# Tiles 0 and 1 of a two-block layer: normalise before the transpose, k weights in two row halves, and an order of work written as a table

## The chip, the cores and the metric

The kernel runs on one core of one Trainium2 chip. The metric is the time of one execution on the device in microseconds (us), as a median over runs. The core has five engines with a queue of instructions each: TensorE (PE: matmuls and the transposes that are matmuls with an identity), VectorE (DVE), ScalarE (ACT), GpSimd (POOL) and SyncE (SP), which issues most of the DMAs. Engines meet only through semaphores. Data live in SBUF (128 partitions), and matmul results in the 8 banks of PSUM.

## The reference

2048 rows of 512 bf16 numbers pass through two blocks with a residual each: linear attention with 32 heads of 16, and a gated MLP that mixes along the rows.

```python
def _A_ref(x, wqkv, wo):                     # x is already layer-normalised
    qkv = (x @ wqkv) ...                      # q, k, v in 32 heads of 16
    phi = lambda t: jnp.where(t > 0, t + 1, jnp.exp(t)) + 1e-06
    pq, pk = phi(q), phi(k)
    kv = jnp.einsum('bhsd,bhse->bhde', pk, v)
    z = jnp.einsum('bhsd->bhd', pk)
    num = jnp.einsum('bhqd,bhde->bhqe', pq, kv)
    den = jnp.einsum('bhqd,bhd->bhq', pq, z)[..., None] + 1e-06
    return (num / den) ... @ wo

def _B_ref(x, w_in, w_sp, b_sp, w_out):      # x is already layer-normalised
    z = _gelu(x @ w_in); z1, z2 = z[..., :896], _layernorm(z[..., 896:])
    g = jnp.einsum('ts,bsf->btf', w_sp, z2) + b_sp[None, :, None]
    return (z1 * g) @ w_out

h = x + _A_ref(_layernorm(x), wqkv, wo)
out = h + _B_ref(_layernorm(h), w_in, w_sp, b_sp, w_out)
```

## The kernel before

The 2048 rows are 16 tiles of 128. Everything stays in SBUF between the blocks. The program is written as a list of operations (`op`), each with an engine, what it reads and writes, a cost that a planner uses, and a due time `want`. `schedule` then goes through a model of the five engines and the DMA queue, and on each engine takes as next the operation with the smallest sum of possible start and half its due time; the due times are a list of 729 numbers (`WANT`) that replaces those written in the code. So the order of each engine's queue comes from the planner before the program is built. `fillers` then puts dummy matmuls with constants (L578) in front of those early matmuls for which the planner sees TensorE idle for more than 0.35 us, up to the first outer product. `waits` places the semaphores.

The order of the work at the start, which is what the change touches:

- SP loads x tile 0, tile 1, tiles 2 and 3, then the k columns of `wqkv` ("wk", 512 rows by 512, in one DMA of 512 KB), three more pairs of x tiles, the q columns ("wq"), one transposing load of the spatial weights `w_sp` (L1043), two DMA transposes of normalised tiles ("tx", L675), the last three pairs of x tiles, and so on.
- VectorE takes mean and variance of each x tile (L590, L594). ScalarE turns the variance into 1/std with Ln and Exp (L605, L607). VectorE, for some tiles ScalarE, writes the normalised tile `xn` (L617, L625).
- Tiles 0 and 1 (`LATE`) are special. VectorE only subtracts their mean (`xc`, L657). TensorE transposes the centred tile (L686), ScalarE and VectorE copy a half each out of PSUM (L691, L693), TensorE multiplies the transposed tile with the k weights (L747), and 1/std comes in as the scale by row of ScalarE's Exp and Relu (L716, L722). Their normalised `xn` is written too, later; a DMA transpose puts it into `xT`, where the q projection reads it.
- Tiles 2 and 3 (`PE_X`) are normalised, transposed on TensorE (L635) and copied by ScalarE (L701). Their 1/std is worked out for both in one pair of instructions. Tiles 4 to 15 are normalised and transposed by DMA (L675), whose result TensorE multiplies with the k weights (L758).
- The feature map of k: Exp and Relu on ScalarE, then minimum and sum on VectorE (L718, L724). `xk` (L768) adds, over all tiles, the products of `xn` with it into 4 banks of PSUM. q (L860) is computed for groups of four tiles: the first group reads the transposed tiles 0 to 3 and the q weights.

Behind this come the sums by head (L780), the product with the v and output weights (L813, L829), the output of the attention (L905, L912) with its division by way of a reciprocal that DMAs spread over partitions (L886) and that VectorE applies (L892), the second normalisation, the two halves of the MLP's first product (L968, L1023), the mixing along rows (L1063) and the last product with its residual (L1083, L1087, stores L1090).

A DMA's queue is served in the order of its issues. `dma_start` on SP or on ScalarE each has a queue of its own; before, ScalarE's is used only for one of the last stores. A tile that VectorE or ScalarE writes for a DMA transpose must be complete before SP issues it, and all that stands behind it on SP waits along.

## Time and profile before

| | us |
|---|---|
| median of 3 runs | 242.42 |
| lowest, highest | 241.86, 245.08 |
| span of the profiled execution, first to last instruction | 240.8 |
| TensorE busy in it | 235.3 |
| VectorE busy | 127.1 |
| ScalarE busy | 83.9 |
| first transpose on TensorE starts | 4.84 |
| first k matmul starts | 6.80 |
| first q matmul starts | 13.04 |

The profiled execution's own time is known by its span alone, 240.8 us, which is 1.62 us under the median. In the profile "PE" is TensorE's matmuls and "PEld" its weight loads, which run beside them. "SPq" and "ACTq" are the issues of DMAs. A row of a timeline gives start and length in us, engine, line, operation, output and input, how many instructions are merged in it, and in brackets how long the engine idled before and what ended that. Ends of matmuls are modelled: a row of several ends later than the next can start. A line number is that of the kernel before unless it is said to be the changed kernel's.

### The profile page before, as it was taken

The page shows a single profiled execution, that of the slowest core. Times are in us where ns is not written, and L with a number is a line of the kernel's source. Part 1 is how long each engine was busy: PE and PEld are TensorE (multiplying, and loading weights), DVE is VectorE, ACT ScalarE, POOL GpSimd, SP SyncE. Part 2 cuts the span into 40 slices and gives each one's busy share as a digit, 9 for nine tenths or more (in the row PEclk, how much of TensorE's full clock was granted, in tenths as well). Part 3 has the DMA queues.
Part 4 walks back from the last instruction along what each step waited for, and adds up shares of the span by engine and source line. Part 5 has one row for each costly group of instructions (what it writes and reads, how often), then busy time and mean ns, then how long its engine had stood idle before and what let it go on. Part 6 is the DMA issues. An engine that isn't in the chain of part 4 may idle for free.

```text
span 240.8 us, 3056 instructions
## 1 busy us (share of the span) xinstructions
PE 235.3 (98%) x1177; PEld 108.4 (45%) x1199; DVE 127.1 (53%) x269; ACT 83.9 (35%) x132; POOL 13.9 (6%) x33
## 2 busy tenths in 40 slices
PE   8999999999999999999999999999999999999996
PEld 2434445454344544444444444444444444444443
DVE  4999856399999983226222333324333433322443
ACT  4888975566065799994111100000000000000000
POOL 3000000000102160213000000000000000000000
PEclk9999999999999999999999999999999999999999
DMA  6986559632542555444444449463300001000022
GB/s 197 254 224 91 109 114 355 207 112 81 145 125 44 92 107 101 97 88 89 109 92 104 88 92 237 108 89 88 109 0 0 25 22 44 0 3 0 0 87 87
DMA packets 61805, 24.18 MB, mean 100 GB/s; under 512 B 52064, under 2 KB 61152, under 8 KB 61792
## 3 DMA queue, kind: packets, MB, share of 16 engines
q1 hardware_dynamic: 61648, 23.97, 41.3%
q8 instruction: 9, 0.15, 0.3%
q10 hardware_dynamic: 144, 0.03, 0.1%
q14 instruction: 4, 0.03, 0.1%
HBM read 7.47 MB, written 2.10 MB: 40 GB/s over the span
## 4 chain that ended last, share of the span: by engine, by line
PE 87%; DMA 5%; DVE 3%; ACT 2%; SPq 1%; issue 1%; ACTq 0%
PE ps L1063 40%; PE ps L1083 10%; PE ps L968 10%; PE ps L1023 10%; PE ps L768 4%; PE ps L860 4%; DMA xT_pq_z<-k_xn_z 4%; PE ps L905 3%; PE ps L758 3%; PE ps L578 2%; DMA wsp<-e 1%; ACT e L716 1%; SPq L886 1%; DVE xT_pq_z L727 1%; ACT k_xn_z L836 1%
## 5 line engine op out<-in xcount | busy, mean ns | idle before, releaser
L1063 PE MATMUL ps<-wsp,k_xn_z 128*128 128x512 bf16 x328 | 73.6, 379 | 0.4
L1069 DVE TENSOR_TENSOR e<-ps,e 128x512 bf16<-128x512 f32 x28 | 19.4, 692 | 69.2 <-PE ps L1063 69.2
L1063 PEld LDWEIGHTS ps<-wsp,k_xn_z 128*128 128x128 bf16 x336 | 32.8, 98 | 39.8 <-issue 0.4
L1023 PE MATMUL ps<-hT,win 128*128 128x512 bf16 x110 | 26.0, 379 | 0.1
L968 PE MATMUL ps<-win,hT 128*128 128x384 bf16 (+1 forms) x126 | 25.3, 352 | 0.1
L1083 PE MATMUL ps<-wout,xT_pq_z 128*128 128x512 bf16 (+2 forms) x125 | 25.1, 355 | 0.1
L1063 PE MATMUL ps<-wqkv_wsp,k_xn_z 128*128 128x512 bf16 x110 | 24.2, 379 | 0.1
L1028 ACT ACTIVATE xT_pq_z<-ps 128x1024 bf16<-128x1024 f32 x14 | 14.1, 1023 | 25.6 <-PE ps L1023 25.5
L590 DVE BATCH_NORM_STATS2 small<-xh 128x6 f32<-128x512 bf16 x32 | 21.0, 679 | 3.1 <-DMA xh<-in_A_x_dram 3.0
L968 PEld LDWEIGHTS ps<-win,hT 128*128 128x128 bf16 x128 | 12.5, 98 | 12.4
L1083 PEld LDWEIGHTS ps<-wout,xT_pq_z 128*128 128x128 bf16 x126 | 11.8, 98 | 12.7
L1063 PEld LDWEIGHTS ps<-wqkv_wsp,k_xn_z 128*128 128x128 bf16 x112 | 11.0, 98 | 13.2
L1023 PEld LDWEIGHTS ps<-hT,win 128*128 128x128 bf16 x112 | 10.9, 98 | 12.7 <-DVE xh L924 0.3
L1087 DVE TENSOR_TENSOR e<-ps,xh 128x512 bf16<-128x512 f32 (+2 forms) x18 | 11.4, 633 | 9.7 <-PE ps L1083 9.2
L716 ACT ACTIVATE e<-ps 128x1024 bf16<-128x1024 f32 (+1 forms) x16 | 15.4, 973 | 2.4 <-PE ps L860 1.2
L860 PE MATMUL ps<-xT_pq_z,wqkv_wsp 128*128 128x512 bf16 x61 | 15.0, 379 | 0.6 <-DMA xT_pq_z<-k_xn_z 0.5
L768 PE MATMUL ps<-k_xn_z 128*128 128x512 bf16 x63 | 15.2, 379 | 0.2 <-issue 0.2
L975 ACT ACTIVATE k_xn_z<-ps 128x896 bf16<-128x896 f32 x12 | 10.9, 909 | 8.8 <-PE ps L968 8.8
L905 PE MATMUL ps<-k_xn_z,xT_pq_z 128*128 128x512 bf16 x58 | 13.3, 380 | 0.3 <-DVE xT_pq_z L892 0.3
L758 PE MATMUL ps<-wqkv_wsp,xT_pq_z 128*128 128x512 bf16 x55 | 13.2, 379 | 0.2 <-ACT xT_pq_z L701 0.2
L1071 DVE TENSOR_TENSOR xT_pq_z<-xT_pq_z,e 128x512 bf16<-128x512 bf16 x28 | 11.9, 425 | 2.2 <-ACT xT_pq_z L1028 1.3
L979 ACT ACTIVATE e<-k_xn_z 128x896 bf16<-128x896 bf16 x12 | 11.4, 951 | 0.3
(77 smaller groups left out, 169.4 us busy)
## 6 DMA issues: line engine op xcount, KB each, us to landing
wsp<-e SPq DMA_DIRECT2D x16, 128.0 KB
out_dram<-e SPq DMA_DIRECT2D x15, 128.0 KB, 1.7
xh<-in_A_x_dram SPq DMA_DIRECT2D x7, 256.0 KB, 3.8
win<-in_B_w_in_dram SPq DMA_DIRECT2D x1, 1792.0 KB, 7.3
wqkv_wsp<-in_A_wqkv_dram SPq DMA_DIRECT2D x3, 512.0 KB, 7.2
wout<-in_B_w_out_dram SPq DMA_DIRECT2D x1, 896.0 KB, 5.5
wsp<-in_B_w_sp_dram SPq DMA_TRANSPOSE x48, 2.6
wqkv_wsp<-in_A_wo_dram SPq DMA_DIRECT2D x1, 512.0 KB, 5.2
```

Source lines behind the costliest of these rows:

```text
L590: op("dve", (0.577, 0.69), lambda e: e.bn_stats(row[0:6].ap(), src.ap()), r=[src], w=[row[0:6]], want=want, name=name)
L716: first = op("act", act_c(n, ptr=len(pt)), lambda e: e.activation(e_(ev).ap(), src(t), ACT.Exp, scale=sc), r=[t()] + pt, w=[e_()], want=wa ...
L758: i = e.matmul(t(bank(ti)).ap(), lhsT=lhs.ap()[:, c, :], rhs=rhs.ap()[:, c, :], start=(c == 0), stop=(c == KD - 1))
L768: i = e.matmul(HT(bank(j)).ap(), lhsT=xn[n, j * P:(j + 1) * P].ap(), rhs=pk[n, :].ap(), start=(n == 0), stop=(n == NT - 1))
L860: k = e.matmul(t(bank(i)).ap(), lhsT=lhs.ap()[:, c, :], rhs=rhs.ap()[:, c, :], start=(c == 0), stop=(c == KD - 1))
L905: i = e.matmul(t(bank(ti)).ap(), lhsT=l.ap()[:, c, :], rhs=mw[c, :].ap(), start=(c == 0), stop=(c == KD - 1 and not unit))
L968: k = e.matmul(t(bank(i)).ap()[:, 0:b - a], lhsT=l.ap()[:, c, :], rhs=win[c, a:b].ap(), start=(c == 0), stop=(c == KD - 1))
L1023: k = e.matmul(t(bank(i)).ap(), lhsT=l.ap()[:, c, :], rhs=r_.ap()[:, c, :], start=(c == 0), stop=(c == KD - 1))
L1028: op("act", act_c(1024), lambda e: e.activation(d.ap(), t(None if same else flat).ap(), ACT.Gelu_apprx_tanh), r=[t()], w=[d], want=want + ...
L1063: k = e.matmul(t(bank(0)).ap(), lhsT=l.ap()[:, s - a, :], rhs=r_.ap()[:, s - a, :], start=(s == 0), stop=(s == NT - 1))
L1069: op("dve", dve_c(512), lambda e: e.tensor_tensor(gb().ap(), t(bank(0)).ap(), bsp().ap()[:, tg * GW:(tg + 1) * GW], ALU.add), r=[t(), bsp( ...
L1083: k = e.matmul(t(bank(0)).ap()[:, 0:r_.ap().shape[-1]], lhsT=l.ap()[:, fc, :], rhs=r_.ap()[:, fc, :], start=(fc == 0), stop=(fc == KF - 1))
```

## The change

- Tiles 0 and 1 (now `FIRST`) are no longer centred only. Each is normalised by VectorE as soon as ScalarE has its 1/std; the normalised tile is transposed on TensorE, and the two copies out of PSUM go into `xT` itself. The buffers `xc` and `xcT`, the two centring instructions, the scale by row in Exp and Relu, and the two DMA transposes of tiles 0 and 1 go.
- 1/std of tiles 2 and 3 is worked out for each by itself (one pair of ScalarE instructions more).
- The k weights come in two DMAs of 256 KB, a row half each ("wka", "wkb"): the first on ScalarE's queue, behind the table load in ScalarE's order and ahead of all else there, the second on SP behind x tiles 0 to 3. k of tiles 0 and 1 is two operations, one for each half.
- The planner no longer chooses: the order of each engine is a table (`ORDER`) of operation numbers. The model behind it, from which the number of fillers and the places in PSUM follow, has other constants for DMAs.
- By the table, these places change. On SP: wkb, tiles 6 and 7, tiles 4 and 5, wq, then the other four pairs of x tiles, two loads of `w_sp`, then the DMA transposes of tiles 4, 5, 7, 6, the v weights (they stood behind the MLP's first weights before), and those of 10, 11, 8, 9, 15, 12, 14, 13; the output weights come after five of the spreading DMAs. On TensorE: 9 fillers, transpose of tile 0, 1 filler, transpose of tile 1, k of tile 0, transpose of tile 2, k of tile 1, transpose of tile 3, k of 2 and 3, xk of tile 0, then half of the first q, xk of tile 1, the other half, xk of tile 2, k of 4 and 5 (before: 9 fillers, transposes of 0 and 1 with 2 fillers between, k of 0 and 1, transposes of 2 and 3, 1 filler, k of 2 and 3, xk of 0, all of the first q, xk of 1 and 2, k of 4 and 5). From the middle of the attention on, single operations change places with a neighbour; from the MLP's first product on, TensorE's order is the same but for tiles 2 and 3 changing places.

```diff
-    LATE = (0, 1)
+    FIRST = (0, 1)
-    LN1 = [[0], [1], [2, 3], [4, 5, 6, 7], [8, 9, 10, 11], [12, 13, 14, 15]]
+    LN1 = [[0], [1], [2], [3], [4, 5, 6, 7], [8, 9, 10, 11], [12, 13, 14, 15]]
...
-    load("sp", "wk", wqkv[:, D:2 * D], w3[:, :, D:2 * D], D * D * 2, -29)
+    load("act", "wka", wqkv[0:2, D:2 * D], w3[:, 0:2, D:2 * D], D * D, -29)
+    load("sp", "wkb", wqkv[2:4, D:2 * D], w3[:, 2:4, D:2 * D], D * D, -29)
...
-                op("dve", dve_f(512), lambda e, n=n, d=d, m=m: e.tensor_scalar(d.ap(), x[n, :].ap(), m.ap(), None,
-                                                                              op0=ALU.subtract),
-                   r=[x[n, :], m], w=[d, cT[n]()], want=T1(n) - 3, name=f"xc{n}")
...
-                                  xc[n][c * P:(c + 1) * P].ap(), ident.all().ap())
+                                  xn[n, c * P:(c + 1) * P].ap(), ident.all().ap())
...
-        d0, d1 = xcT[n][0:2, :], xcT[n][2:4, :]
+        d0, d1 = xT[0:2, n * P:(n + 1) * P], xT[2:4, n * P:(n + 1) * P]
...
-        dma_t(xn[n, :], xT[:, n * P:(n + 1) * P], 12, f"tx{n}")
...
-        first = op("act", act_c(n, ptr=len(pt)), lambda e: e.activation(e_(ev).ap(), src(t), ACT.Exp, scale=sc),
+        first = op("act", act_c(n), lambda e: e.activation(e_(ev).ap(), src(t), ACT.Exp),
...
-            lhs = xcT[n].all() if n in LATE else xT[:, n * P:(n + 1) * P]
...
+            halves = ((0, 2), (2, 4)) if n in FIRST else ((0, 4),)
+            for a, b in halves:
+                l, rhs = xT[a:b, n * P:(n + 1) * P], wqkv[a:b, D:2 * D]
...
-    g.schedule()
+    g.schedule(ORDER)
```

More of the change, by code (lines that the diff above doesn't have):

```diff
@@ L149, in ready, with schedule @@
         return p.done
-    def schedule(self):
+    def schedule(self, table):
+        queue = {e: [self.ops[i] for i in table[e]] for e in self.ENGINES}
+        assert sorted(i for e in self.ENGINES for i in table[e]) == list(range(len(self.ops)))
+        assert all(o.eng == e for e in self.ENGINES for o in queue[e])
         for o in self.ops:
@@ L235, in schedule @@
                     o.done = t_end + 0.3
[L236 to L240 removed]
+                elif o.eng == "act":
+                    a_beg = max(t + LAG, a_end)
+                    a_end = a_beg + o.nbytes / SHARE
+                    o.done = a_end + LAND
+                else:
+                    c_end = max(t + LAG, c_end, t_end + 1.2)
+                    left_ = o.nbytes
+                    for until, rate in ([(a_end, SHARE)] if c_end >= a_beg - 0.3 else []) + RATES:
+                        if left_ > 0 and c_end < until:
+                            k = min(left_, (until - c_end) * rate)
+                            c_end += k / rate
+                            left_ -= k
+                    o.done = c_end + LAND
             for tl in o.tiles:
@@ L253, in schedule @@
                 last = o
-            order[o.eng].append(o)
-            cand[o.eng].remove(o)
-            for u in users.get(o, ()):
-                need[u] -= 1
-                if not need[u]:
-                    cand[u.eng].append(u)
             left -= 1
-        self.order = order
+        self.order = queue
         self.span = max(o.done for o in self.ops)
@@ L1101, in build @@
     g.outs = outs
-    if WANT is not None:
-        for o, w in zip(g.ops, WANT):
-            o.want = w * UNIT
     return g
```

143 lines of the change are left out of this document (60 added, 83 removed), and 73 rows, old and new, of tables (ORDER, WANT).

## The prediction

> **What bounds the kernel now.** I read the page first: engines, then the chain that ended last.
>
> ```profile
> PE 235.3 (98%) x1177; PEld 108.4 (45%) x1199; DVE 127.1 (53%) x269; ACT 83.9 (35%) x132; POOL 13.9 (6%) x33
> ...
> PE 87%; DMA 5%; DVE 3%; ACT 2%; SPq 1%; issue 1%; ACTq 0%
> ```
>
> TensorE is busy for 98% of a 240.8 us span and makes 87% of the chain. The matrix work is not changed, so only time in which TensorE idles or runs fillers can be won. The windows view says where that lies (columns: stretch, length, then busy time and instructions by engine).
>
> ```profile
> 0.00:4.83 4.83, 4.00 (x9) 1.18 (x10) 1.84 (x6) 1.79 (x4) 2.01 (x13) 1.00 0.56 153
> ...
> 6.80:13.04 6.24, 5.58 (x32) 2.34 (x30) 6.22 (x21) 5.92 (x14) 0.00 (x0) 1.00 1.26 250
> 13.04:54.00 40.96, 40.59 (x264) 18.96 (x269) 29.56 (x62) 29.27 (x41) 0.00 (x0) 1.00 0.66 171
> 54.00:65.00 11.00, 10.57 (x53) 4.37 (x51) 10.36 (x18) 4.86 (x7) 0.96 (x2) 1.00 0.36 112
> 65.00:238.60 173.60, 172.69 (x818) 80.62 (x832) 76.94 (x162) 41.21 (x66) 10.93 (x18) 1.00 0.32 73
> ```
>
> From 13.04 us on TensorE idles 0.37, 0.43 and 0.91 us, mostly cracks of 0.05. What can be won lies before 13.04. There VectorE is busy 6.22 of 6.24 us and ScalarE 5.92. TensorE's timeline and the list of its waits:
>
> ```profile
> 0.83 4.00 PE L578 MATMUL ps<-const-bfloat16-1.0 128*128 128x512 bf16 x9 [0.83 <-PEq L1174]
> 4.84 0.59 PE L686 MATMUL ps<-small,hn 128*128 128x128 bf16 x4
> 5.22 1.06 PE L578 MATMUL ps<-const-bfloat16-1.0 128*128 128x512 bf16 x2
> 6.40 0.59 PE L686 MATMUL ps<-small,hn 128*128 128x128 bf16 x4
> 6.80 1.91 PE L747 MATMUL ps<-wqkv_wsp,hn 128*128 128x512 bf16 x8
> 8.68 0.72 PE L635 MATMUL ps<-small,k_xn_z 128*128 128x128 bf16 x8
> 9.24 0.38 PE L578 MATMUL ps<-const-bfloat16-1.0 128*128 128x512 bf16 x1
> 9.77 1.90 PE L758 MATMUL ps<-wqkv_wsp,xT_pq_z 128*128 128x512 bf16 x8 [0.15 <-ACT xT_pq_z L701]
> 11.50 1.03 PE L768 MATMUL ps<-k_xn_z 128*128 128x512 bf16 x4
> 13.04 3.61 PE L860 MATMUL ps<-xT_pq_z,wqkv_wsp 128*128 128x512 bf16 x15 [0.51 <-DMA xT_pq_z<-k_xn_z]
> ...
> 20.80 1.89 PE L758 MATMUL ps<-wqkv_wsp,xT_pq_z 128*128 128x512 bf16 x8
> ```
> ```profile
> PE ps L860 <- DMA xT_pq_z<-k_xn_z: 0.5, 1, 0.5
> PE ps L905 <- DVE xT_pq_z L892: 0.3, 1, 0.3
> ```
>
> L686 are the transposes of tiles 0 and 1, L747 k of both, L635 and L758 the same of tiles 2 and 3, L768 the first outer product (xk0), L860 q of the first group. From the first k matmul to q, 6.24 us pass, with 20 matmuls and 8 transposes in them: 20 x 0.216 ((11.50 - 9.77) / 8) + 0.56 (8.68 to 9.24) = 4.88. So 1.36 us are lost there: a wait for xn2, a filler, 0.15 for a copy, and 0.51 at 13.04 for the DMA transposes of tiles 0 and 1, which only the change removes.
>
> **The change, part by part.** The rows that set the start:
>
> ```profile
> 0.79 1.28 ACT L572 ACT_TABLE_LOAD   x1 [0.79 <-PEq L1174]
> ...
> 2.96 0.69 DVE L590 BATCH_NORM_STATS2 small<-xh 128x6 f32<-128x512 bf16 x1 [2.96 <-DMA xh<-in_A_x_dram]
> 3.69 0.18 DVE L594 BATCH_NORM_AGGREGATE small<-small 128x2 f32<-128x6 f32 x1
> ...
> 3.91 0.30 ACT L605 ACTIVATE small<-small 128x1 f32<-128x1 f32 x1 [1.83 <-DVE small L594]
> 4.23 0.20 ACT L607 ACTIVATE small<-small 128x1 f32<-128x1 f32 x1
> ...
> 4.37 0.33 DVE L657 TENSOR_SCALAR hn<-xh,small 128x512 bf16<-128x512 bf16 x1
> ...
> 5.47 0.29 DVE L693 COPY hn<-ps 128x256 bf16<-128x256 bf16 x1
> 5.67 0.41 DVE L617 TENSOR_SCALAR k_xn_z<-xh,small 128x512 bf16<-128x512 bf16 x1
> 6.00 0.35 DVE L657 TENSOR_SCALAR hn<-xh,small 128x512 bf16<-128x512 bf16 x1
> ...
> 7.03 0.29 DVE L693 COPY hn<-ps 128x256 bf16<-128x256 bf16 x1
> ...
> 7.32 0.38 DVE L617 TENSOR_SCALAR k_xn_z<-xh,small 128x512 bf16<-128x512 bf16 x1
> ...
> 9.11 1.09 ACT L701 ACTIVATE xT_pq_z<-ps 128x512 bf16<-128x512 bf16 x2
> ```
>
> *k weights on two queues.* No run shows two load queues at once. The half on ScalarE's queue leaves beside x0 and shares the DMA engines with it. The rate in the first 5 us, in slices of 0.125 us:
>
> ```profile
> GB/s 0 0 0 0 0 0 0 0 0 0 0 0 0 0 90 115 164 230 279 254 221 287 336 197 123 147 57 172 270 369 369 344 279 213 229 246 303 369 393 377
> ```
>
> 128 KB at the top rate of 393 is 0.33 us: if x0 must let as many bytes of weights pass, it lands up to 0.33 later. It lands no later at all if ScalarE's issue waits behind its table load (0.79 + 1.28), and hardly so if the engines' gaps (57 to 230 GB/s) take the weights in. I take +0.25, nearer the shared end, since both queues are free at 0.79. The Trainium skill ("DMA: Bandwidth & Descriptors", Issuing engines are not separate DMA queues) speaks against a second queue: it says that loads from two engines end on the same 16 DMA engines and interleave, so that only issue time is saved. By that rule the term is the full 0.33; no run here shows it yet. The weights themselves are in time either way: k waits for nothing at 6.80.
>
> *Normalise at once.* Stats at 3.21, aggregate 0.73 later (3.69 - 2.96) at 3.94, ScalarE's Ln and Exp end 0.74 after that (4.23 + 0.20 - 3.69) at 4.68, xn0 4.70 to 5.11 (0.41). Before, the centring needed no ScalarE but stood behind the second stats until 4.37, so tr0 comes at 5.16 in place of 4.84. Copies follow 0.63 later (5.47 - 4.84) at 5.79; xn1 0.20 behind (5.67 - 5.47), 5.99 to 6.40; tr1 at 6.45 (before 6.40: 6.00 + 0.35 + 0.05). k0 then starts 0.40 later, at 6.85 for 6.80: **0.05 lost**. VectorE drops two centrings (0.33 + 0.35) and moves two normalises ahead of them; that brings tile 2 forward. Exp and Relu of tiles 0 and 1 lose their scale by row; I count that at nothing, since TensorE waits there for the copies, not for them. The memsets and masks on GpSimd change places only: its part of the start is 2.01 us long by the first row of the windows, and done before the first Ln wants its constant. The constants of the planner and the table of orders cost no instruction; what they move is counted where it lands.
>
> *Tiles 2 and 3.* Copies of tile 1 at 7.08, xn2 0.29 behind (7.32 - 7.03) to 7.78, tr2 at 7.83, where k0 has ended at 7.71: 0.12 waited. k1 8.11 to 8.97, tr3, k2 at 9.25 to 10.12. ScalarE has one more Ln/Exp pair (0.53) for tile 3, then the first Relu, the copy of tile 2 by about 9.15, and that of tile 3 at 9.6 to 10.2 (0.6 each: 1.09 for two): k3 waits about 0.13, like the 0.15 in the row. k3 and xk0 (0.865 each) end at 11.98. xk0 needs the first feature sum from VectorE by 11.1; I get 11.0.
>
> *No DMA transposes of tiles 0 and 1.* SP's queue:
>
> ```profile
> 6.13 4.08 SPq L675 DMA_TRANSPOSE xT_pq_z<-k_xn_z  x2
> 10.25 1.62 SPq L540 DMA_DIRECT2D xh<-in_A_x_dram  x3
> 11.91 2.45 SPq L1043 DMA_TRANSPOSE wsp<-in_B_w_sp_dram  x2
> 14.41 11.10 SPq L675 DMA_TRANSPOSE xT_pq_z<-k_xn_z  x8
> ```
>
> They held SP for 4.08 us and the last three x loads behind them until 10.25; these now leave right behind wq. q no longer waits for a transpose, only for its weights, which land earlier in the byte order than now. So q starts at 11.98 for 13.04: **1.06 won**.
>
> *Is it kept?* Behind q TensorE is full, so the lead lasts if every supplier moves too. ScalarE's and VectorE's work follows TensorE's and moves with it. The DMA transposes are the close ones. The summary of those issued from 14 to 26 us:
>
> ```profile
> L675 SPq DMA_TRANSPOSE xT_pq_z<-k_xn_z x8: 1264/1272/1761, 14.4 to 24.2; - x8
> ...
> DMA to landing us min/median/max: 2.5/2.8/4.4
> ```
>
> Tile 6 now stands behind tile 7 on SP, and tile 7 behind ScalarE's normalise, which I move by the lead to end at 15.7. Then tile 6 is issued at 17.0 and lands at 19.8 by the median of 2.8, where k6 wants it at 20.80 - 1.06 = 19.74. A landing of 4.4 would cost 1.6; 2.5 costs nothing. I take 0.25, near the median row. wv (512 KB, 1.3 us at 393 GB/s) moves to ahead of tile 10's transpose; that one is issued near 18.8 and even with 4.4 + 1.3 lands at 24.5, 0.4 after its use: in the range, not in the sum. In return kvT finds wv landed. From 54 us on the order differs by single places; the 0.28 wait for a scaled q there depends on ScalarE's chain and moves along: 0.
>
> **Sum:** -1.06 + 0.25 = -0.8 us, in which the 0.05 is contained. The profiled span of 240.8 becomes 240.0. It is 1.6 under the median of the runs, 242.42, which I carry over: 241.6.
>
> **Rivals.**
>
> *The clock comes later, and it ends slower (243.8).* Nine fillers take 4.00 us, 0.43 each; from 6.80 on a matmul takes 0.216. So TensorE got its full clock near 6.8. (The granted clock reads 1.00 in every row of the windows, the first too; the cadence tells more.) Before, it was idle only some 0.15 us between 0.83 and then. Now one filler of the three goes, and it idles from 4.83 to 5.16 and about 0.3 ahead of tr1. If that postpones the clock past k0 and k1, these 8 matmuls cost 0.21 more each and the transposes 0.23 more per four (0.59 against 0.36): 1.7 + 0.46 = 2.2, and 241.6 + 2.2 = 243.8. It decides from four slow matmuls on. For it: twice or more the idle time. Against it: gaps of 0.3 among 6 us. The Trainium skill ("TensorE: Matmul & The Clock Gate", Part 1) says that the clock is raised after a busy window of 3.4 us that runs free of the kernel's start; by that rule a missed window would hold some 12 matmuls at the slow cadence, 2.5 us and 244.1, by estimate. The cadence in the rows agrees that there is such a step; its window no row shows.
>
> *The lead is spent on transposes (242.3).* If tile 6 or 10 lands late as in the slow rows, 0.7 to 1.0 of the lead goes into waits at k6 or k10. For it: zero slack at tile 6 by the median. Against it: SP itself is ahead by over a microsecond.
>
> *x0 is not delayed (241.2).* Then all of the start stands 0.25 earlier, and the transposes of tiles 4 to 7 with it. This is the change doing less on the second queue than it says, and better for it.
>
> **How the numbers follow.** Forecast 0.55 with its own range 241.0 to 242.0; x0 undelayed 0.13; lead spent 0.15; late clock 0.14; other 0.03. The range 240.7 to 243.5 leaves out the worst of the late clock and the remainder. About 2% (4.8 us) is what a measurement of this kernel tells from no change. Ahead of the first q 13.04 - 4.88 = 8.2 us are no matrix work, and 4.84 of them pass before the first transpose can start, which the change does not shorten; at most 3.3 are to be won, so faster by over 2% has 0.01. Slower by over 2% needs the late clock through all 20 matmuls (20 x 0.21 = 4.2) and more: 0.04. Within 2%: 0.95.
>
> **What would show it.** First stats near 3.2 us; tr0 near 5.2 and k0 near 6.85; no DMA wait in front of the first q, which starts near 12.0; k6 near 19.8 to 20.0 with a short wait for a transpose. It is wrong if the first q starts after 12.7, if matmuls still take 0.43 after 7 us, or if TensorE shows new waits of over half a microsecond between 15 and 54 us.

## The result, and the profile after

The changed kernel took 244.14 us (median of 22 runs, 242.31 to 247.78) beside 242.25 (22 runs, 241.6 to 245.08) for the kernel before on the same chip: a ratio of 1.0068, interval 1.0043 to 1.0093. Forecast were 241.6 us and a small gain. It became slower by about 0.7%, which lies within the 2% called "same", and the median lies above the forecast range. The ratio leaves out the slowest run of the changed kernel (247.78), which is over 1.5% above its quickest.

The runs of the changed kernel fall into groups. Nine of 22 have a mean granted clock under 1.00: eight at 0.993 (244.03 to 245.93 us) and one at 0.986. The other 13 stand between 242.31 and 245.5, their median at 243.41. A mean of 0.993 over 242 us is 3.4 us at half clock. The profiled execution (242.56 us) is one of the quick ones, with a clock of 1.00, and its span is 240.8 us, the same as before.

Its stretches, cut as in the prediction (length, then busy time and instructions of TensorE, its weight loads, VectorE, ScalarE, GpSimd; granted clock, DMA share, GB/s):

```profile
0.00:4.83 4.83, 4.00 (x9) 1.19 (x9) 1.40 (x3) 1.78 (x3) 1.89 (x12) 1.00 0.61 182
4.83:6.80 1.97, 0.84 (x8) 0.54 (x8) 1.97 (x8) 0.94 (x4) 0.00 (x0) 1.00 0.94 285
6.80:13.04 6.24, 6.24 (x37) 2.76 (x36) 6.24 (x22) 6.12 (x17) 0.00 (x0) 1.00 1.19 306
13.04:54.00 40.96, 40.33 (x263) 18.35 (x261) 28.96 (x60) 28.76 (x40) 0.00 (x0) 1.00 0.67 156
54.00:65.00 11.00, 10.75 (x55) 4.35 (x53) 10.40 (x17) 4.94 (x7) 1.06 (x3) 1.00 0.35 110
65.00:238.60 173.60, 173.53 (x834) 80.70 (x831) 77.00 (x162) 41.02 (x66) 10.92 (x18) 1.00 0.33 73
```

Between 6.80 and 13.04 TensorE now runs without a gap. In return it is busy only 0.84 of the 1.97 us ahead of that, and between 13.04 and 54 it idles 0.63 us, where it idled 0.37. Its timeline at the start and the list of its waits in this kernel (columns as in the prediction):

```profile
0.82 4.00 PE L583 MATMUL ps<-const-bfloat16-1.0 128*128 128x512 bf16 x9 [0.82 <-PEq L1154]
5.46 0.50 PE L683 MATMUL ps<-small,k_xn_z 128*128 128x128 bf16 x4 [0.64 <-DVE small L599]
5.80 0.38 PE L583 MATMUL ps<-const-bfloat16-1.0 128*128 128x512 bf16 x1
6.68 0.40 PE L683 MATMUL ps<-small,k_xn_z 128*128 128x128 bf16 x4 [0.49 <-DVE k_xn_z L622]
6.91 1.03 PE L741 MATMUL ps<-wqkv_wsp,xT_pq_z 128*128 128x512 bf16 x4
...
11.15 1.04 PE L751 MATMUL ps<-k_xn_z 128*128 128x512 bf16 x4
12.02 1.24 PE L843 MATMUL ps<-xT_pq_z,wqkv_wsp 128*128 128x512 bf16 x5
```
```profile
PE ps L683 <- DVE small L599: 0.6, 1, 0.6
PE ps L683 <- DVE k_xn_z L622: 0.5, 1, 0.5
PE ps L741 <- DMA xT_pq_z<-k_xn_z: 0.3, 1, 0.3
PE ps L888 <- DVE xT_pq_z L875: 0.3, 1, 0.3
PE ps L812 <- DVE hT L805: 0.2, 1, 0.2
```

The first q starts at 12.02, as forecast, 1.02 ahead of before. The wait for DMA transposes in front of it (0.5) is gone. Two idle spells ahead of the transposes of tiles 0 and 1 (0.64 and 0.49) are new. So are waits for tile 10's and 11's DMA transposes at k (L741; 0.24 and 0.49, as the distance between the starts of two matmuls less the 0.216 of one) and a wait at the product with the output weights (L812, 0.38 in that way). All of the lead is gone at the end: both profiled executions end their last matmul at 238.53.

One number serves as a ruler from here on: the span less the start of the first q. It was 240.8 - 13.04 = 227.8 before, and is 240.8 - 12.02 = 228.8 after. One microsecond was won in front of q and one was lost behind it.

A second ruler says where: from the start of the first q to the first matmul of the attention's output at L905 (L888 in the changed kernel), with the same matmuls between. Before and after:

```profile
55.05 2.54 PE L905 MATMUL ps<-k_xn_z,xT_pq_z 128*128 128x512 bf16 x11
```
```profile
55.15 2.75 PE L888 MATMUL ps<-k_xn_z,xT_pq_z 128*128 128x512 bf16 x12
```

That is 42.01 us before and 43.13 after. The waits 0.24, 0.49 and 0.38 are 1.11 of the 1.12 between them.

### The profile page after: what moved, and what is told of

It is laid out like the page before. It is cut to its first block, busy times and chain, and to the rows that moved or that the text cites. A ratio compares the mean times of both kernels' runs of the same rounds, so it can differ in the third digit from the quotient of the medians.

```text
span 240.8 us, 3075 instructions
## 1 busy us (share of the span) xinstructions
PE 235.7 (98%) x1197; PEld 107.9 (45%) x1197; DVE 126.2 (52%) x267; ACT 83.6 (35%) x134; POOL 13.9 (6%) x33
## 4 chain that ended last, share of the span: by engine, by line
PE 88%; DMA 4%; DVE 3%; ACT 2%; SPq 1%; issue 0%
PE ps L1046 40%; PE ps L1006 10%; PE ps L1066 10%; PE ps L951 10%; PE ps L751 5%; PE ps L741 5%; PE ps L843 4%; PE ps L888 3%; DMA xT_pq_z<-k_xn_z 2%; DMA xh<-in_A_x_dram 1%; DMA wsp<-e 1%; ACT e L710 1%; DVE xT_pq_z L875 1%; SPq L869 1%; ACT k_xn_z L819 1%; DVE small L595 1%
## 5 line engine op out<-in xcount | busy, mean ns | idle before, releaser
L951 PE MATMUL ps<-win,hT 128*128 128x512 bf16 (+1 forms) x128 | 25.4, 352 | 0.0
L710 ACT ACTIVATE e<-ps 128x1024 bf16<-128x1024 f32 (+1 forms) x18 | 16.6, 931 | 6.0 <-PE ps L741 3.1
L741 PE MATMUL ps<-wqkv_wsp,xT_pq_z 128*128 128x512 bf16 x64 | 15.3, 379 | 0.4 <-DMA xT_pq_z<-k_xn_z 0.3
L843 PE MATMUL ps<-xT_pq_z,wqkv_wsp 128*128 128x512 bf16 x64 | 15.3, 379 | 0.0
L888 PE MATMUL ps<-k_xn_z,xT_pq_z 128*128 128x512 bf16 x60 | 13.6, 379 | 0.3 <-DVE xT_pq_z L875 0.3
L712 DVE TENSOR_SCALAR e<-e 128x1024 bf16<-128x1024 bf16 (+1 forms) x18 | 6.9, 388 | 10.2 <-ACT e L710 10.2
```

The lines of the kernel that those rows point to most:

```text
L710: first = op("act", act_c(n), lambda e: e.activation(e_(ev).ap(), src(t), ACT.Exp), r=[t()], w=[e_()], want=want, name=name + ".exp")
L741: i = e.matmul(t(bank(ti)).ap(), lhsT=l.ap()[:, c - a, :], rhs=rhs.ap()[:, c - a, :], start=(c == 0), stop=(c == KD - 1))
L843: k = e.matmul(t(bank(i)).ap(), lhsT=lhs.ap()[:, c, :], rhs=rhs.ap()[:, c, :], start=(c == 0), stop=(c == KD - 1))
L888: i = e.matmul(t(bank(ti)).ap(), lhsT=l.ap()[:, c, :], rhs=mw[c, :].ap(), start=(c == 0), stop=(c == KD - 1 and not unit))
L951: k = e.matmul(t(bank(i)).ap()[:, 0:b - a], lhsT=l.ap()[:, c, :], rhs=win[c, a:b].ap(), start=(c == 0), stop=(c == KD - 1))
```

## The experiments

Two theories stood first. The *clock theory*: the idle spells at the start let the granted clock of TensorE come late or go again. The *order theory*: what the new table does behind the first q gives the lead back. A third asked what the second queue costs. "New order" is the table of the change, "old order" that of the kernel before. In kernels with the old order written in, line numbers are 41 lower (L642, L700, L802, L581 for L683, L741, L843, L622).

| kernel | order | fillers ahead of tiles 0, 1 | k weights | first q | span less first q | first q to output | median, us | ratio to before, interval |
|---|---|---|---|---|---|---|---|---|
| before | old | 1, 2 | whole | 13.04 | 227.8 | 42.01 | 242.25 | 1 |
| changed | new | 1, 1 | halves, 2 queues | 12.02 | 228.8 | 43.13 | 244.14 | 1.0068, 1.0043 to 1.0093 |
| 1 | new | 3, 2 | halves, 2 queues | 12.43 | 228.7 | 43.06 | 243.17 | 1.0072, 1.0044 to 1.0100 |
| 2 (before) | old | 0, 0 | whole | 12.13 | 228.6 | 42.03 | 243.88 | 1.0062, 1.0035 to 1.0090 |
| 6 | new | 5, 3 | halves, 2 queues | 12.59 | 229.1 | 43.50 | 243.62 | 1.0062, 1.0033 to 1.0091 |
| 8 | new, output weights early | 5, 3 | whole | 12.47 | 228.9 | 43.44 | 243.25 | 1.0042, 1.0017 to 1.0066 |
| 9 | old | 1, 1 | halves, 2 queues | 14.24 | 227.9 | 42.09 | 243.56 | 1.0061, 1.0030 to 1.0092 |
| 10 | old | 3, 2 | halves, 2 queues | 12.68 | 227.6 | 42.02 | 242.32 | 1.0003, 0.9987 to 1.0020 |
| 13 | old | 3, 2, and 3 at k | whole | 13.09 | 227.8 | 42.02 | 242.06 | 0.9970, 0.9944 to 0.9996 |
| 14 | old | 2, 2, and 1 at k | whole | 12.23 | 227.8 | 42.02 | 241.81 | 0.9979, 0.9956 to 1.0002 |

First q, span and "first q to output" (the second ruler) are those of the one profiled execution of each kernel; medians are of all runs. Kernels were measured on different chips, so medians of different rows differ by that too; each ratio is to the kernel before on the same chip. The kernels left out of the table fit its last ruler: 43.18 to 45.43 in experiments 3, 4, 5 and 11 (new order), 42.01 in experiment 15 (old order).

### The clock: experiments 1, 2 and 6

Experiment 1 adds fillers to the changed kernel, experiment 2 takes them from the kernel before, experiment 6 adds more.

```diff
+    for o in g.order["pe"]:
+        o.fill = {'tr0': 3, 'tr1': 2}.get(o.name, o.fill)     # 1
+        o.fill = {'tr0': 0, 'tr1': 0}.get(o.name, o.fill)     # 2, in the kernel before
+        o.fill = {'tr0': 5, 'tr1': 3}.get(o.name, o.fill)     # 6
```

> The changed kernel with four fillers more: 11 in place of 9 ahead of the first transpose and 2 in place of 1 between the first two, so that TensorE runs through its two idle stretches of 0.64 and 0.66 us; nothing else differs. Clock theory (the idle stretches let the clock fall back or come late in many executions): the median falls from 244.1 to 242.0 to 242.6, close to the changed kernel's best runs of 242.3, every execution has a granted clock of 1.000, and the spread shrinks to that of the kernel before (241.6 to 243). Transposes theory (the loss is the waits at k10, k11 and at the v product, in every execution): it stays at 244 and spread from 242 to 248. Second-queue theory (the loss is x1 landing 0.9 us late): it stays at 244 too.

> The kernel before with the three fillers around its first two transposes taken away (8 in place of 9 ahead of the first, none in place of 2 between them), so that TensorE idles about 0.4 us ahead of the first transpose and 1.0 ahead of the second; nothing else differs. Clock theory: the median rises from 242.25 by 1 to 2 us, to 243.3 to 244.3, and some executions show a granted clock of 0.993. The two other theories: no change, 242.2, since fillers do no work and the chain through VectorE is untouched.

> The changed kernel with 5 fillers ahead of the transposes of tile 0 and 3 ahead of those of tile 1 in place of 1 and 1; nothing else. Clock theory: TensorE idles under 0.6 us ahead of tile 0 and under 0.2 ahead of tile 1 where the clock is granted early, no execution has a granted clock under 1.00 (8 of 22 of the changed kernel had 0.993), and the median falls from 244.1 to between 242.5 and 243.2. Rival (the cause lies in the later waits for transfers alone): the spread over executions stays as it was, about a third at 0.993, median 243.8 to 244.4. Rival (fillers at half clock push the transposes back): tile 0 is transposed at 6.0 or later and the first q starts 0.5 later than the 12.02 of the changed kernel.

Experiment 2 touches nothing but three fillers of the old kernel, and its median rose from 241.96 to 243.88, with half of its 12 runs at 243.9 or more. Idle time of TensorE at the start is enough to make an execution some 2 us longer. How, no trace of this kernel shows: its profiled execution is a quick one that kept its clock, and six of its eight runs above 243.5 read a clock of 0.999 or 1.00. A clock that comes late would read so (experiment 11, below). In experiments 1 and 6 no run has a clock under 0.999, beside nine of 22 of the changed kernel. That fits the theory but does not settle it: on the chips of experiments 1 and 6, kernels with the fillers of the change (3, 4, 5 and 7) have only four such runs of 36, and the kernel before three of 35 on one of them. The pair that settles it, on one chip, is 9 and 10. The ratio did not improve in 1 and 6: the quickest runs moved up, from 242.31 to 242.87 and 243.39, as the first q came 0.4 and 0.6 later and, in 6, L812 waited 0.68. In the new order fillers alone repair nothing.

### Single moves within the new order: experiments 3, 4, 5, 7, 8 and 11

Experiment 3 puts the load of the v weights behind the spatial weights, much as the kernel before has it. Experiment 4 puts both halves of the k weights on SP. Experiment 5 issues the output weights ahead of the first spread. Experiment 7 loads the k weights whole, on SP. Experiment 8 is 5, 6 and 7 together. Experiment 11 moves tile 10's normalisation forward.

```diff
# 3: v weights (88) late
-        101, 102, 104, 103, 88, 107, ... 525, 526, 527, 222,
+        101, 102, 104, 103, 107, ... 525, 526, 527, 88, 222,
# 4: first half of the k weights (1) on SP
-        20, 1, 24,           0, 3, 4, 2,
+        20, 24,              0, 3, 4, 1, 2,
# 5: output weights (89) ahead of the spreads
-        525, 526, 527, 222, 223, 224, 221, 262, 89, 261,
+        525, 526, 527, 89, 222, 223, 224, 221, 262, 261,
# 7: k weights whole
-    load("act", "wka", wqkv[0:2, D:2 * D], w3[:, 0:2, D:2 * D], D * D, -29)
-    load("sp", "wkb", wqkv[2:4, D:2 * D], w3[:, 2:4, D:2 * D], D * D, -29)
+    load("sp", "wk", wqkv[:, D:2 * D], w3[:, :, D:2 * D], D * D * 2, -29)
# 11: on VectorE the sums of tiles 8 to 11 (58 to 64) ahead of the first q's map (211, 212), tile 10 (70) behind it; on ScalarE 1/std (65, 66) ahead of Exp (215)
-        57, 211, 131, 212, 58, 64, 62, 60, 135, 216, 67, 137, 217, 70, 72,
+        57, 58, 64, 62, 60, 211, 131, 212, 67, 70, 135, 216, 137, 217, 72,
```

> The changed kernel with the load of the v weights moved on SP from ahead of tile 10's transpose to behind the MLP's first weights, ahead of the first spreading DMA, much as in the kernel before. Transposes theory: the waits of 0.24 and 0.27 us at k10 and k11 go, the lead over the kernel before lives on past 26 us, and median and lowest time both fall by about 0.5 us (243.6 and 241.8). Clock theory: the median stays near 244 with the same share of executions at 0.993, only the lowest may fall by 0.3. Second-queue theory: 244.1, nothing.

> The changed kernel with both halves of the k weights on SP's queue, in order behind x tiles 0 to 3, and none on ScalarE's. Second-queue theory: x1 lands at 3.37 in place of 4.29 and x2 at 4.6 in place of 5.4, the first transpose starts at 4.9 to 5.1 in place of 5.47, and the median falls to 242.0 to 242.6. Clock theory: the idle stretch ahead of the first transpose shrinks from 0.64 to about 0.2 us, the one ahead of the second stays near 0.5, so part of the loss goes: 242.8 to 243.6, still with some executions at 0.993. Transposes theory: 244, unchanged.

> The changed kernel with one load moved: the output weights are issued right behind the third spatial-weight transpose of their group, ahead of the first spread of group 0, instead of between two spreads of group 2 (issue at about 41 us instead of 47.9). Theory A (the load lands after its user is ready): it lands near 47, the 0.38 us wait ahead of the product L812 is below 0.1, and the last matmul of a comparable execution ends 0.3 to 0.4 earlier (238.2 instead of 238.53), median down by that, to about 243.8. Rival B (that wait is for the vector engine's masked copy at L805, as the page names it): the wait stays at 0.38 and nothing moves. Rival C (the stage from 57 to 70 us, where the vector engine is the last to end, takes the gain back): the wait goes and the end stays within 0.1 of 238.53.

> The changed kernel with the k weights in one transfer on the sync queue behind the third load, as in the kernel before; the rest of the change stays (1 filler ahead of each of tiles 0 and 1). Theory A (two halves cost transfer time of their own: the second half landed at 6.90 with the second queue and at 7.91 with both halves on one, where the whole landed at 6.47): the whole lands between 6.4 and 6.7, x1 lands near 3.37 and x2 near 4.62, transposes of tile 0 at 5.0, k of tile 0 at 6.5 without a wait of 1 us, first q at 11.6 to 11.9. Rival B (the time of the k weights is set by what else moves at 5 to 8 us): it lands at 7.5 or later and k of tile 0 waits for it as with two halves on one queue, first q 12.2 or later. The median by A: 0.2 to 0.4 below that of the changed kernel; the clock stays as uneven as it was.

> The three edits of the other kernels of this call together: output weights ahead of the spreads, 5 and 3 fillers, the k weights in one transfer. If the clock and the two late transfers are what the change loses by, and the gains add up, the first q starts at 11.7 to 12.2, the wait ahead of L812 is gone, no clock under 1.00 appears, and the median is 241.4 to 242.0, under the kernel before by 0.1 to 0.7. If the stage from 57 us on takes the lead back, it is 242.2 to 242.8, no better than the kernel before. Median over 243.5: the clock theory is wrong.

> The changed kernel with one step moved: the sums of tiles 8 to 11 on the vector engine ahead of the first q's feature map, their square root on ScalarE ahead of the second exponential of q, and the normalisation of tile 10 two operations after the first feature map, instead of behind the second. Theory A (tile 10's place in the vector engine's order makes the waits of k of tiles 10 and 11): it is ready at about 17.5 instead of 20.04, its transpose is issued at about 18.85 instead of 20.06, and the waits of 0.24 and 0.49 us ahead of k of tiles 10 and 11 shrink to under 0.1 each; the wait ahead of the output weights' product stays or grows to 0.8, because that transfer's issue is tied to a spread. Rival B (the v weights' transfer, issued ahead of it and landing at 23.6, sets it): the transpose lands at 23.9 or later and at least 0.4 us of the two waits remains. The median falls by at most 0.3 by A, not at all by B.

None of them brought the kernel back. Experiment 3: 246.02 (1.0175, 1.0150 to 1.0199). The wait at tile 11 went and that at tile 10 grew to 0.45, but the MLP's first weights (win) landed at 45.4 for 42.4 and the output weights at 54.58 for 51.99, and L812 waited 2.98 us; no theory had foreseen that. Experiment 4: 244.35 (1.0094, 1.0062 to 1.0125). x1 and x2 land early again (3.37 and 4.64), but the second half of the weights lands at 7.91, and k waits for it in the middle of tile 0 (TensorE's timeline in that kernel):

```profile
6.53 0.59 PE L741 MATMUL ps<-wqkv_wsp,xT_pq_z 128*128 128x512 bf16 x2
7.96 0.60 PE L741 MATMUL ps<-wqkv_wsp,xT_pq_z 128*128 128x512 bf16 x2 [0.83 <-DMA wqkv_wsp<-in_A_wqkv_dram]
```

Experiment 5: 244.63 (1.0075, 1.0044 to 1.0106). The output weights land at 47.93, yet L812 waits longer, 0.60. VectorE's rows in this kernel show the reason:

```profile
49.02 1.29 DVE L787 CAST hT<-ps 128x512 bf16<-128x512 f32 x2 [0.71 <-PE ps L751]
51.21 1.29 DVE L875 TENSOR_TENSOR xT_pq_z<-xT_pq_z,wsp 128x1024 bf16<-128x1024 bf16 x2 [0.91 <-DMA wsp<-e]
52.42 0.42 DVE L805 TENSOR_TENSOR hT<-ps,small 128x256 bf16<-128x256 f32 x1
```

The spreads now queue behind the weights in the DMA, VectorE waits 0.91 for them, and the masked copy (L805) that L812 needs stands behind that on VectorE. Whichever of the two transfers goes first, the other is late. Experiment 7 alone (243.85; 1.0052, 1.0018 to 1.0085) is not settled; its profiled execution (246.54, clock 0.993) is one of its three slowest, so nothing is read from it. In experiment 8, with all three edits, the whole k weights land at 7.08, no clock is under 1.00, the waits at tiles 10 and 11 (0.38, 0.47) and at L812 (0.34) are all still there, and so is the ruler at 228.9. Experiment 11: 245.3 (1.0128, 1.0086 to 1.0171); tile 10 was normalised at 18.79, but its transpose was issued at 20.26, right behind the v weights, and landed 5.60 later. The waits at tiles 10 and 11 fell only from 0.73 to 0.58, and a new one of 1.8 us came at the attention's output (L888). In its profiled execution the clock never came before 10 us; TensorE's timeline has k of tile 0 at 0.43 us a matmul:

```profile
6.86 0.61 PE L683 MATMUL ps<-small,k_xn_z 128*128 128x128 bf16 x4 [0.28 <-DVE k_xn_z L622]
7.26 1.91 PE L741 MATMUL ps<-wqkv_wsp,xT_pq_z 128*128 128x512 bf16 x4
```

Four of them take 1.91 there, and 1.03 in the changed kernel's profile.

### The old order on the changed computation: experiments 9 and 10

Experiment 9 keeps all that the change computes, with its fillers, both queues and halves, and replaces the table `ORDER` by the order that the kernel before had on each engine. Experiment 10 is the same with 3 and 2 fillers.

```diff
-ORDER = { ... the table of the change ... }
+ORDER = { ... the kernel before's order; tx0, tx1, xc0, xc1 left out, xn0 and xn1 in the place of xc0 and xc1 ... }
```

> The changed kernel's computation (tiles 0 and 1 normalised at once, k weights in two row halves, one on ScalarE's queue, 1 filler ahead of each of tiles 0 and 1), but with the kernel before's order of work written into the table on every engine, the removed operations left out. Theory A (the start's lead is real and the new order behind the first q loses it: the normalised tile 10 is ready at 20.04 instead of 18.64, its transposes and the spreads come late): tile 10 is normalised by 18.2, no wait over 0.15 us for transposed tiles 10 and 11, the wait ahead of the product with the output weights is gone, and the quickest executions are at 241.2 to 241.8. With the clock theory the executions spread as those of the kernel before without fillers did (241.8 to 245.1), median 242.3 to 243.7. Rival B (the second queue and the halves cost at the start what the normalisation gains): first q at 12.9 or later, quickest execution over 242.0. Rival C (the stage after 57 us takes any lead back): the lead of 0.5 to 1.0 us holds to 60 us and the end is within 0.2 of 238.5.

> The same kernel in the kernel before's order with 3 fillers ahead of tile 0 and 2 ahead of tile 1. Theory A and the clock theory together: no execution under a clock of 1.00, first q between 12.0 and 12.6, median 241.5 to 242.1, level with or a little under the kernel before. If the fillers do nothing: same median as the run without them, 242.3 to 243.7. If the lead is lost somewhere that neither order nor clock explains: median 242.6 or more with a clock of 1.00 in every execution.

Experiment 9 has the ruler of the old kernel, 227.9, and the clock's trouble in plain sight. TensorE's timeline and the windows of that kernel:

```profile
0.82 3.51 PE L542 MATMUL ps<-const-bfloat16-1.0 128*128 128x512 bf16 x9 [0.82 <-PEq L1113]
5.51 0.39 PE L642 MATMUL ps<-small,k_xn_z 128*128 128x128 bf16 x4 [1.17 <-DVE small L558]
...
6.92 0.47 PE L642 MATMUL ps<-small,k_xn_z 128*128 128x128 bf16 x4 [0.82 <-DVE k_xn_z L581]
7.18 3.55 PE L700 MATMUL ps<-wqkv_wsp,xT_pq_z 128*128 128x512 bf16 x8
```
```profile
3.40:6.80 3.40, 1.54 (x9) 0.48 (x7) 2.74 (x9) 1.29 (x5) 0.00 (x0) 1.00 0.93 283
6.80:10.20 3.40, 3.27 (x12) 1.36 (x13) 2.78 (x11) 2.22 (x7) 0.00 (x0) 0.55 1.24 314
```

The clock was granted early here, while the spin still ran, so nine fillers took 3.51 us and were used up at 4.3. Then TensorE idled 1.17 and 0.82. The clock went, eight k matmuls took 3.55 us in place of 1.9, and the first q started at 14.24. The same windows of experiment 10:

```profile
3.40:6.80 3.40, 2.67 (x15) 0.99 (x14) 3.07 (x10) 1.29 (x5) 0.00 (x0) 1.00 0.94 274
6.80:10.20 3.40, 3.02 (x22) 1.34 (x21) 3.00 (x10) 2.90 (x9) 0.00 (x0) 1.00 1.21 335
```

With TensorE busy 2.67 of the 3.40 us the clock stayed, and in all 12 runs it reads 1.00, where experiment 9 has five of 12 at 0.993. (Experiment 10 missed its own marks narrowly: first q at 12.68, median 242.32.) The four corners are then: new order with 1 and 1 fillers 1.0068, with 3 and 2 1.0072; old order with 1 and 1 1.0061, with 3 and 2 1.0003. Either fault alone costs some 0.6 to 0.7%; the kernel is back where it was only when both are mended. The two do not add up: both together cost no more than one, and why is open. In the old order the fillers' effect (1.0030 to 1.0092 beside 0.9987 to 1.0020) is shown, and so is the order's effect with 3 and 2 fillers (1.0044 to 1.0100, six runs, beside 0.9987 to 1.0020).

### What part of the order, and what the second queue is worth: experiments 12 to 15

Experiment 12 takes the new order with 3 and 2 fillers and the old one on SP alone, from the first DMA transposes on. Experiment 13 is the old order with the k weights whole on SP: of the change, only the earlier normalisation is left (and 1/std of tiles 2 and 3 each by itself). Experiment 15 repeats 13, experiment 14 has fewer fillers.

```diff
# 12: SP behind the two spatial-weight transposes 522 and 529
-        101, 102, 104, 103, 88, 107, 108, 105, 106, 112, 109, 111, 110, 523, 524, 528, 90, 525, 526, 527, 222, 223, 224, 221, 262, 89, ...
+        101, 102, 103, 104, 107, 108, 106, 105, 524, 527, 528, 109, 110, 111, 112, 90, 525, 523, 526, 89, 88, 223, 221, 222, 224, 261, ...
# 13 and 15, beside the table and the load of experiment 7
+        o.fill = {'tr0': 3, 'tr1': 2, 'k0.0': 3}.get(o.name, o.fill)
# 14
+        o.fill = {'tr0': 2, 'tr1': 2, 'k0.0': 1}.get(o.name, o.fill)
```

> The changed kernel with 3 and 2 fillers, its own order on TensorE, the vector engine, ScalarE and GpSimd, and on the sync queue its own order up to the first two spatial-weight transposes, then the kernel before's (v weights behind the output weights, both ahead of the spreads). Measured by the time from the first q to the last matmul, which was 225.3 to 225.5 with the old order and 226.4 to 226.5 with the new: theory S (the sync queue's order loses it): 225.4 to 225.7, no wait at the product with the output weights, none at k of tile 11, median 242.2 to 242.6. Theory V (the vector engine's place of tile 10 loses it): its normalisation stays at about 20.2, k of tile 10 still waits 0.3 us or more, the interval stays at 226.0 or more, median 242.9 or more.

> Of the change only the normalisation ahead of the transposes: the kernel before's order on every engine, the k weights in one transfer on the sync queue as before, 3, 2 and 3 fillers ahead of tile 0, tile 1 and the first k. If the second queue and the halves are worth something (k of tile 0 can start on the first half): the whole k weights land at 6.5 to 7.5, the first k starts at 6.9 or later, the first q 0.2 to 0.5 later than the 12.68 of the run with halves, median 242.4 to 242.8. If they cost (x1 and x2 land 0.9 and 0.5 later by the second queue): x1 at 3.4, transposes of tile 1 at 6.1, first q at 12.2 to 12.5, median 241.6 to 242.1, at or under the kernel before.

> Normalisation ahead of the transposes alone, the kernel before's order, k weights whole, with 2, 2 and 1 fillers ahead of tile 0, tile 1 and the first k in place of 3, 2 and 3. If the fillers at half clock held the transposes up: tile 0 is transposed near 5.1 instead of 5.47, the first q starts at 12.3 to 12.8 instead of 13.09, every clock stays at 1.00, median 0.2 to 0.5 under that of the run with 3, 2 and 3. If fewer fillers let the clock slip: some executions over 243.5, median 242.2 or more. If neither: the two medians within 0.15.

> The kernel with 3, 2 and 3 fillers once more, as the reference of this call: median 241.9 to 242.2, every execution with a clock of 1.00, ratio to the kernel before 0.995 to 1.001.

Experiment 12 came out at 244.82 (1.0077, 1.0047 to 1.0108). The marks of theory V were met: tile 10 is normalised at 20.24 and k of tile 10 waits 0.37. But L812 no longer waits, as theory S had it, and the ruler is 230.4, 1.7 above experiment 1, because other waits came:

```profile
PE ps L733 <- DMA xT_pq_z<-k_xn_z: 1.0, 4, 0.3
...
PE ps L943 <- DVE small L591: 0.9, 1, 0.9
```

One queue's order from one table does not fit the rest from the other, so no single queue can be named as the one that loses the microsecond. Experiments 13 and 15 are at 0.9970 and 0.9987 (0.9966 to 1.0008), level with the kernel before or a little under it, and experiment 14 at 0.9979. In 13 the first q came 0.41 later than in 10, as the theory in favour of the halves had it. But the whole weights had landed at 6.37, and with fewer fillers (14) the first q came at 12.23: it was the fillers that held 13 up. The start in experiment 14:

```profile
0.82 4.42 PE L542 MATMUL ps<-const-bfloat16-1.0 128*128 128x512 bf16 x10 [0.82 <-PEq L1115]
5.04 0.63 PE L642 MATMUL ps<-small,k_xn_z 128*128 128x128 bf16 x4
5.47 0.75 PE L542 MATMUL ps<-const-bfloat16-1.0 128*128 128x512 bf16 x2
6.38 0.40 PE L642 MATMUL ps<-small,k_xn_z 128*128 128x128 bf16 x4 [0.16 <-DVE k_xn_z L581]
...
12.23 2.11 PE L802 MATMUL ps<-xT_pq_z,wqkv_wsp 128*128 128x512 bf16 x9
```

TensorE is never idle over 0.16 us ahead of k, the first q starts 0.81 before that of the kernel before, and the span is 240.0 for 240.8: the lead arrives at the end in full. Its median is 241.81 beside 242.35 of the old kernel and 242.12 of experiment 15 on the same chip; its interval still touches 1. The halves and the second queue bring nothing that can be measured (experiment 10 beside 13, 14 and 15). What they add is in the loads alone: k of tiles 0 and 1 was two operations, one for each half of the rows, in the kernel before too.

## Why the prediction was wrong, step by step

**The start: right, in part by luck.** k0 was forecast at 6.85 and came at 6.91, k2 at 9.25 and came at 9.24, the first q at 11.98 and came at 12.02. But the transposes of tiles 0 and 1 came 0.30 and 0.23 late (5.46 for 5.16, 6.68 for 6.45). k0 made that up because TensorE had its full clock by tile 1 in this execution: the row of that transpose is 0.40 long for 0.59 before, and k0 followed 0.23 behind its start, where 0.40 was forecast.

**The second queue: right in the sum, wrong in the place.** x0 was to land 0.25 later; it landed 0.09 later (0.23 in experiment 10). What the first half of the weights held up were the loads behind it on SP: x1 landed at 4.29 for 3.37, x2 at 5.37 for 4.62. The rule of the Trainium skill ("DMA: Bandwidth & Descriptors", Issuing engines are not separate DMA queues) holds: the loads share the engines. The prediction drew from it only what it means for x0. VectorE's rows in the changed kernel, and behind them those of experiment 14:

```profile
4.31 0.69 DVE L595 BATCH_NORM_STATS2 small<-xh 128x6 f32<-128x512 bf16 x1 [0.35 <-DMA xh<-in_A_x_dram]
4.92 0.40 DVE L622 TENSOR_SCALAR k_xn_z<-xh,small 128x512 bf16<-128x512 bf16 x1
```
```profile
3.74 0.66 DVE L554 BATCH_NORM_STATS2 small<-xh 128x6 f32<-128x512 bf16 x1
4.42 0.41 DVE L581 TENSOR_SCALAR k_xn_z<-xh,small 128x512 bf16<-128x512 bf16 x1
```

Tile 1's stats stand ahead of tile 0's normalisation on VectorE. They waited 0.35 for x1, and so tile 0 is normalised at 4.92, where 4.70 was forecast and 4.42 is what experiment 14 shows without the second queue. The transpose of tile 0 came at 5.46 for 5.16.

**"Is it kept?": the step that failed.** The prediction said that VectorE's and ScalarE's work follows TensorE's and moves with it, and charged 0.25 for tile 6. Tile 6 made no wait at all. TensorE's suppliers did not all move with it. The loss came at tiles 10 and 11, which the prediction left to the range and to the rival *the lead is spent on transposes* (0.7 to 1.0 us, chance 0.15), and at the output weights, whose later place among the spreads it did not price. VectorE's rows before, and then after:

```profile
18.23 0.41 DVE L617 TENSOR_SCALAR k_xn_z<-xh,small 128x512 bf16<-128x512 bf16 x1
...
19.22 1.22 DVE L727 SCALAR_TENSOR_TENSOR xT_pq_z<-ps,e 128x1024 bf16<-128x1024 f32 x1
```
```profile
18.50 1.22 DVE L721 SCALAR_TENSOR_TENSOR xT_pq_z<-ps,e 128x1024 bf16<-128x1024 f32 x1
19.63 0.41 DVE L622 TENSOR_SCALAR k_xn_z<-xh,small 128x512 bf16<-128x512 bf16 x1
```

VectorE's own feature map of the second half of q is 0.72 earlier. But the table has put the normalisation of tile 10 behind it instead of ahead, so that comes 1.40 later. SP issued its transposes at 20.06, where the prediction had 18.8, behind the v weights (512 KB, issued at 18.24, landed at 23.63). SP's queue in the changed kernel, and behind it three pieces of its chain (start, length, what):

```profile
18.24 0.58 SPq L544 DMA_DIRECT2D wqkv_wsp<-in_A_wqkv_dram  x1
20.06 5.71 SPq L672 DMA_TRANSPOSE xT_pq_z<-k_xn_z  x4
```
```profile
21.30 4.36 DMA xT_pq_z<-k_xn_z
25.66 0.05 issue
25.71 1.04 PE ps L741 x4
```

Tile 11's transpose took 4.36 us from issue to landing, and k waited for it. Tile 10's took 4.15 and landed at 24.22, the very moment at which it landed in the kernel before; TensorE was ready for it at 24.11, where it had come at 25.12. The v weights are not what makes that transpose slow. It took as long with no load near it before, and with the v weights moved away in experiment 3 (pieces of the chains of both):

```profile
19.81 4.41 DMA xT_pq_z<-k_xn_z
```
```profile
20.35 4.36 DMA xT_pq_z<-k_xn_z
```

Why it is slow in these kernels is open. For tile 11 the v weights may be to blame: 4.36 with them, 3.64 before, 2.49 in experiment 3.

0.24 and 0.49 at tiles 10 and 11, and up to 0.38 at L812, make the 1.1 by which the second ruler grew. That ruler stands at 42.01 to 42.09 in the seven profiles with the old order, at 43.06 and more in the eight with the new that are read here. That the order loses the lead is shown; how the loss divides between tile 10's place and the two weight loads is read from the waits alone, and the single moves did not separate it. The first ruler, the whole span less first q, is less sharp: 227.6 to 228.1 in experiments 9, 10, 13, 14 and 15, but 228.6 in experiment 2. There a lead of 0.91 came whole through the attention and went behind it, 0.34 of it in a wait for the second normalisation (L968). The lead of experiment 14 lasts to the end.

**"The clock comes later": a rival that came, in another form.** It had a chance of 0.14 and the price of 2.2 us (243.8). It spoke of a clock that is granted late; the 0.993 of the changed kernel's runs and the trace of experiment 9 are a clock that was granted and went again. No such execution of the changed kernel itself was profiled. The runs with a clock of 0.993 have a median of 244.82, those with 1.00 243.41: 1.4 apart. Experiment 2 puts it at 1.9 in the median. So the price was about right, a little high, and the chance was too low by far. The prediction also took this rival and the spent lead for alternatives; both came, in the same kernel. The prediction weighed gaps of 0.3 ahead of the two transposes; they were 0.64 and 0.49, and 1.17 and 0.82 where the clock came early and the fillers ran off quicker, which it had not thought of. The Trainium skill ("TensorE: Matmul & The Clock Gate", Part 1) has a free-running window of 3.4 us. The trace agrees with the length: in experiment 9 the granted clock reads 0.56, 0.50, 0.50 and 0.73 in the four microseconds from 7 to 11, which is 3.4 us at half clock. The prediction's estimate of such a window, 12 slow matmuls and 2.5 us, does not follow: at 0.43 each, 3.4 us hold eight, which cost 1.7 us more than at full clock, and the eight of experiment 9 lost 3.55 - 1.9. The Trainium skill's advice on the same page (Why this matters for your kernels), to avoid idle gaps over some 3 us, would let gaps of 0.5 to 1.2 us pass; experiment 9 shows that 1.17 and 0.82 can be enough, and the measurement decides. They are not enough every time: in the profiled executions of experiments 2 and 5 the clock stayed over gaps of 0.37 and 1.01, and of 0.61 and 1.18.

**The medians.** The prediction carried 1.6 us from the span to the median. The changed kernel's profiled execution has 240.8 and 242.56, 1.76 apart, so that step was sound for one quick run. The median of all its runs lies another 1.58 above. The clock makes part of that (the 13 runs at 1.00 have 243.41); what spreads those 13 is left open. A clock that came late, which reads as 1.00, may be part of it.

## What to carry to other kernels

A lead won at the start is worth what the tightest supplier behind it lets through: follow each engine's order up to the next shared wait, and price every load that changed its place, before counting the lead as kept. Dummy matmuls are not idle time to be won: check that they cover the gap also when the clock comes early and they run at twice the rate. When a change comes with a new order of work, put the old order on the new computation first; here that run, with enough fillers, gave the kernel before's time back within 0.2%.

## What the runs showed of the hardware that was not expected

- The clock can go on gaps of about a microsecond: 1.17 and 0.82 us of idling, with TensorE busy 1.54 of 3.40 us, were enough in experiment 9; at 1.93 (experiment 2), 2.02 (5), 2.33 (1) and 2.67 of 3.40 (10) it stayed. That is one execution of each.
- The granted clock in the profile counts a clock that goes again, not one that comes late for the first time: in experiment 11 k's matmuls stand 0.43 us apart up to 10 us, and every window of it there reads 1.00.
- 256 KB on a second queue held up the loads behind it on the first by 0.92 and 0.75 us, and the first load by only 0.09 (experiment 10: 1.01, 0.52 and 0.23).
- One DMA transpose issued between 18 and 22 us took 4.0 to 4.6 us to land in the kernel before and in experiments 2, 3, 9, 10, 13 and 14, where most took 2.4 to 2.6. No load stands between it and the transposes ahead of it in the queue; the reason is open.
